# Five small moves in the hand-written order of a chunked recurrence with a maxout feed-forward: a DMA queue, a range check, a key transpose, a block of products and a weight difference

## The chip, the cores and the metric

The kernel runs on one core of one Trainium2 chip. The metric is the device time in microseconds (us) of that core. A core has five instruction streams: TensorE (PE), VectorE (DVE), ScalarE (ACT), GpSimd (POOL) and SyncE (SP). Each works through its own instructions in order. DMAs are started by instructions in such a stream; in the profile "SPq" and "ACTq" are the DMA-starting instructions of SP and ACT.

## The reference

```python
# attention: B, H, S, D = 4, 8, 768, 48
f = 1.0 / (1.0 + np.exp(-f_logit))
for t in range(S):
    state = f[:, :, t, :, None] * state + np.einsum('bhd,bhe->bhde', k[:, :, t], v[:, :, t])
    y[:, :, t] = np.einsum('bhd,bhde->bhe', q[:, :, t], state)
x = y.transpose(0, 2, 1, 3).reshape(B * S, H * D)          # 3072 x 384
# feed-forward: w1, w2, w3 are 384 x 768, w_out is 768 x 384
h = np.maximum(np.maximum(x @ w1, x @ w2), x @ w3)
out = h @ w_out
```

All inputs arrive as given by the host; the four weights come in double precision and are rounded on the chip.

## The kernel before

**Units and groups.** The recurrence is cut into 24 units of 64 time steps by two batches (128 rows of x each), numbered 0 to 23. Four units make a group of 512 rows, and the feed-forward runs group by group, six in all, one group behind the recurrence. The main loop (L1071) takes one unit u per turn, from 4 to 23. Between the steps of a turn, `fill` (L967) draws pieces of the pending feed-forward from a generator until a budget of TensorE time is used up. So one written-out order interleaves two jobs on every engine, and no scheduler changes it.

**One turn of the loop.** For unit u the turn holds: `keys(u)` (L362, four TensorE transposes of the scaled keys and a ScalarE copy, for units below 6 only) or `keys_by_blocks` (L372, 16 VectorE transposes, for the later units); `values(u-1)` (L403) and `sums(u-1)` (L424) on TensorE; `pairs(u)` (L389: 16 products on TensorE, L396, which read the scaled keys kh and queries qh of u, then a masked copy on VectorE, L399); `finish(u-1)` (L496: 16 products at L504, then three ScalarE copies at L511 into the feed-forward's input xT); the loads of later units; then the scans of unit u+1 on VectorE (L329, L347) with GpSimd's products L340 (kh) and L351 (qh).

**Loads.** From unit 6 on, f, k and q of two units are loaded together, 8 DMAs each (`load`, L183), and v of one unit by two DMAs of 96 KB (`load_v`, L164). All go through SP. In the turn of unit u, `load_v(u + 2)` follows `finish(u-1)`.

**The first group.** `ffn_first` (L797) also rounds the weights, turns the first weight, multiplies it with w_out (`linear`, L783), and before and after that moves rows of the weights between partitions: `place` (L454) starts ten DMAs for each of two `placed` tiles (L458, L465: placed<-w_in) and ten more for a third (w_in<-w_in), all on SP. GpSimd then forms sums of the placed weights, `mix_in` (L844, L850), and four differences of w_out, `mix` (L588, L592), of which `mix(1)` writes over a corner of w_out that the first group's output products (L568) still read.

**The later groups.** `inputs_by_pairs` (L869) works by a scheme with seven products instead of eight per pair of blocks. For each of three parts n it has `start`, `plain`, `sixth`, `fifth`, `seventh`, `third` and `fourth`; each adds products (L881) to one of two accumulators, A[n] in a bank of `ps_f` (p in the profile), B[n] in a bank of `ps_tr` (tr). After some of them ScalarE copies the accumulator out: L895 after start, L889 after plain, L909 after sixth, L904 after fifth. The accumulator can't be added to again before its copy is done. `sixth(0)` needs t2 and `fifth(0)` t1, which GpSimd makes in `sums_of_x` (L856, L865) from xT, once two small DMAs (`pack`, L519, L524: xT<-xT) have put the last rows of the group in place.

**Range check.** `check_range` (L273) looks, in three ScalarE steps a turn, whether the weights lie in a range: step 0 takes absolute values (L278), steps 1 and 2 are at L280. It runs from unit 10 on.

**How DMAs wait.** In the build every DMA counts up one of eight semaphores (DMAHW0 to DMAHW7) when it has landed, and a DMA instruction first waits until the DMA before it on its semaphore, in the order of the build, has landed. SP's and ACT's DMAs share the eight. A wait holds the stream it stands in.

Of the kernel before, what the change touches and what calls it, by code (L numbers as in the profile page):

```python
# [55 lines left out]
def kernel(  # L56
# [21 lines left out]
    GRP = 4  # L78
# [11 lines left out]
    def fast():  # L90
        ctx = ExitStack()
        with ctx:
# [64 lines left out]
            one = (nc.sync, nc.sync)  # L157
            both = (nc.sync, nc.scalar)
            act = (nc.scalar, nc.scalar)
# [28 lines left out]
            def load_v(u, queues=one):  # L188
                load_tokens(v_tiles[u % NLD], v, u, queues)
# [558 lines left out]
            def store_late():  # L748
                while late:
                    store(*late.pop(0))  # L750
# [46 lines left out]
            def ffn_first(xT):  # L797
                hm = new_hm()
                steps = [(j, slice(n * HALF, (n + 1) * HALF)) for n in range(2) for j in range(J_HALF)]
                steps += [(j, slice(0, TOK)) for j in range(J_HALF, NJ)]  # L800
                n_step = 0
                for j, t in steps:
                    w = t.stop - t.start
                    for i in (1, 2):
                        p = yield from product(xT, j, i, t)
                        if i == 1:
                            nc.scalar.copy(hm[:, j, t], p)
                        else:
                            nc.vector.scalar_tensor_tensor(hm[:, j, t], hm[:, j, t], 0.0, p, op0=ALU.max, op1=ALU.max)
                        round_to(ROUNDED[n_step])  # L810
                        load_weights(2, rounded[0] - 1)
                        yield (1 if w == TOK else NK) * w * COLUMN
                        n_step += 1
                        if n_step in TURNED:
                            yield from turn(TURNED[n_step])
                for a in range(NK):
                    if a < 2:
                        for n in range(2 * NK + 2):
                            place(placed[a].bitcast(FP32), w_in[a + 1], n)
                    for cost in linear(a):  # L820
                        round_to(rounded[0] + 1)
                        yield cost
                for n in range(2 * NK + 2):
                    place(w_lin, w_nat, n)
                made = iter([lambda n=n: mix_in(n) for n in range(4)] + [lambda: mix(0)])
                for i in range(GRP):
                    for n, cost in enumerate(outputs(hm, xT, i)):
                        if i or n:
                            next(made, lambda: None)()
                        if i == GRP - 1 and n == 1 and 1 in packed:  # L830
                            sums_of_x(1)
                        if i == GRP - 1 and n == 2:
                            for k in range(1, 4):
                                mix(k)
                        yield cost

# [15 lines left out]
            packed, summed = {}, {}  # L852
# [16 lines left out]
            def inputs_by_pairs(g, hm, xT):  # L869
                X = lambda k, h: halves(xT, k, h)  # L870
                t1, t2, t3, t4, t5 = sums_of_x(g)
                s1, s2, s4 = w_sum
                s3 = w_two[1][:, 0]
                COST = 2 * HALF * COLUMN
                out = lambda n, h: hm[:, 2 * n:2 * n + 2, h * HALF:(h + 1) * HALF]
                first, u3 = rests[:, 0:2, 0:HALF], tops[:, 2:4, 0:HALF]
                A, B, U5 = {}, {}, {}

                def into(b, n, w, x, begin=False):
                    for j in range(2):  # L880
                        nc.tensor.matmul(b[:, j * HALF:(j + 1) * HALF], lhsT=w[:, (2 * n + j) * 128:(2 * n + j + 1) * 128],  # L881
                                         rhs=x, start=begin and j == 0, stop=True, skip_group_check=True)

                def plain(n):
                    B[n] = bank(True)
                    into(B[n], n, w_two[0][:, 1], X(1, 0), True)
                    yield COST
                    into(B[n], n, w_two[0][:, 2], X(2, 0))
                    nc.scalar.copy(out(n, 0), two(B[n]))  # L889
                    yield COST  # L890

                def start(n):
                    A[n] = bank()
                    into(A[n], n, w_two[0][:, 0], X(0, 0), True)
                    nc.scalar.copy(first, two(A[n]))  # L895
                    yield COST

                def join(n):
                    nc.gpsimd.tensor_tensor(out(n, 0), out(n, 0), first, op=ALU.add)

                def fifth(n):
                    into(B[n], n, s1, t1, True)
                    U5[n] = two(new_top(TOK))
                    nc.scalar.copy(U5[n], two(B[n]))  # L904
                    yield COST

                def sixth(n):
                    into(A[n], n, s2, t2)
                    nc.scalar.copy(out(n, 1), two(A[n]))  # L909
                    yield COST  # L910

                def seventh(n):
                    into(A[n], n, s3, t3)
                    yield COST
                    into(A[n], n, w_two[1][:, 2], X(2, 1))
                    nc.scalar.copy(u3, two(A[n]))
                    nc.gpsimd.tensor_tensor(u3, u3, U5[n], op=ALU.add)
                    yield COST

                def third(n):  # L920
                    into(B[n], n, s4, X(1, 1))
                    yield COST
                    into(B[n], n, w_two[0][:, 2], X(2, 1))
                    nc.vector.tensor_tensor(out(n, 1), two(B[n]), out(n, 1), op=ALU.add)  # L924
                    yield COST

                def fourth(n):
                    into(A[n], n, w_two[1][:, 1], t4)
                    yield COST
                    into(A[n], n, w_two[1][:, 2], t5)  # L930
                    nc.vector.scalar_tensor_tensor(out(n, 0), out(n, 0), 0.0, two(A[n]), op0=ALU.max, op1=ALU.max)
                    nc.vector.scalar_tensor_tensor(out(n, 1), out(n, 1), 0.0, u3, op0=ALU.max, op1=ALU.max)  # L932
                    sums_of_hm(hm, n)
                    if g == 1:
                        for i in ((0, 1), (2, 3, 4), ())[n]:
                            mix_x(i)
                    yield COST

                yield from start(0)
                yield from plain(0)  # L940
                join(0)
                store_late()
                yield from sixth(0)
                yield from fifth(0)
                for n in range(1, NJ // 2):
                    yield from plain(n)
                    yield from seventh(n - 1)
                    yield from start(n)
                    join(n)
                    yield from third(n - 1)  # L950
                    yield from fifth(n)
                    yield from sixth(n)
                    yield from fourth(n - 1)
                yield from seventh(NJ // 2 - 1)
                yield from third(NJ // 2 - 1)
                yield from fourth(NJ // 2 - 1)
# [10 lines left out]
            def fill(ns):  # L967
                budget[0] += ns
                while budget[0] > 0 and pending:
                    try:  # L970
                        budget[0] -= next(pending[0])
                    except StopIteration:
                        pending.pop(0)
# [10 lines left out]
            CHECKS = 2 * GRP + 2  # L984
# [7 lines left out]
            with tc.manual_schedule():  # L992
# [78 lines left out]
                for u in range(GRP, NU):  # L1071
# [2 lines left out]
                    if n == BY_ROWS:  # L1074
                        scan(n)
                    fill(part)
                    keys(u)
                    keys_by_blocks(u, 2)
                    room_of_unit = room_of_pairs()
                    if u > GRP:  # L1080
                        values(u - 1)
                        sums(u - 1, room_of_unit)
                    pairs(u, room_of_unit)
                    if u > GRP:
                        finish(u - 1, xT)
# [12 lines left out]
                    if BY_ROWS <= u + 3 < NU and u % 2:  # L1098
                        load(u + 3, one, "fkq" if u % GRP == 1 else "f")
                    if u + 2 < NU:  # L1100
                        load_v(u + 2)
                    keys_by_blocks(u, 3)
                    if n < NU:
                        if n < BY_ROWS:
                            sigmoids(n)
                        if n != BY_ROWS:
                            scan(n)
                    check_range(u - CHECKS, 0)
                    fill(part)
                    if n < NU:  # L1110
                        after(n)
                        before(n)
                    fill(part)
                    if BY_ROWS < u + 2 < NU and u % GRP == 0:
                        load(u + 2, one, "k")
# [289 lines left out]
```

## Time and profile before

| What | Value |
|---|---|
| Time, median of 3 runs | 415.52 us (415.32 to 416.43) |
| The profiled execution's own time | 416.13 us |
| Its span in the trace | 414.4 us, TensorE clock 0.999 |
| PE busy | 393.5 us (95%) |
| DVE, POOL, ACT busy | 295.1, 246.0, 180.4 us |
| PE in 180 to 240 us | 59.62 of 60.00 us busy |
| PE in 110 to 170 us | 10.00, 9.18, 9.40, 10.00, 8.47, 9.30 of each 10.00 us |
| PE in 360 to 414 us | 49.40 of 54.00 us busy |

The span is what the trace covers; 1.7 us of the profiled execution's own time lie outside it. From about 180 us to 360 us TensorE hardly ever stands still, so a change there must shorten TensorE's own waits of some tenths. The waits of a microsecond and more lie in the first 40 us, in 120 to 165 us, where the first group of the feed-forward goes over to the second, and at the end.

In the timelines a line gives the start and the time taken in us, the engine, the source line, what is written and read, the number of instructions merged into it (a float32 product counts as two), and in brackets how long the engine stood idle before it and whom it waited for.

### The profile page before, as it was taken

The page shows a single profiled execution, that of the slowest core. Times are in us where ns is not written, and L with a number is a line of the kernel's source. Part 1 is how long each engine was busy: PE and PEld are TensorE (multiplying, and loading weights), DVE is VectorE, ACT ScalarE, POOL GpSimd, SP SyncE. Part 2 cuts the span into 40 slices and gives each one's busy share as a digit, 9 for nine tenths or more (in the row PEclk, how much of TensorE's full clock was granted, in tenths as well). Part 3 has the DMA queues.
Part 4 walks back from the last instruction along what each step waited for, and adds up shares of the span by engine and source line. Part 5 has one row for each costly group of instructions (what it writes and reads, how often), then busy time and mean ns, then how long its engine had stood idle before and what let it go on. Part 6 is the DMA issues. An engine that isn't in the chain of part 4 may idle for free.

```text
span 414.4 us, 11516 instructions
## 1 busy us (share of the span) xinstructions
PE 393.5 (95%) x4598; PEld 331.8 (80%) x4598; DVE 295.1 (71%) x569; ACT 180.4 (44%) x430; POOL 246.0 (59%) x270
## 2 busy tenths in 40 slices
PE   5988999999999989999999999999999999999995
PEld 4766765556667878998889988899988889988994
DVE  6997896997785899898899997998995550002600
ACT  2488786421223522335532345532445424586110
POOL 2189694830969777567495296577377860435700
PEclk9999999999999999999999999999999999999999
DMA  8999886676356766277645276735374003542002
GB/s 168 238 271 272 246 228 90 85 139 161 84 103 99 122 108 124 57 96 114 114 123 109 43 112 85 148 87 89 60 144 110 2 17 88 133 133 72 0 21 62
DMA packets 181562, 47.21 MB, mean 114 GB/s; under 512 B 160448, under 2 KB 179200, under 8 KB 181504
## 3 DMA queue, kind: packets, MB, share of 16 engines
q1 hardware_dynamic: 178032, 45.62, 54.1%
q10 hardware_dynamic: 3472, 0.81, 0.9%
q8 instruction: 37, 0.61, 0.6%
q14 instruction: 21, 0.17, 0.1%
HBM read 37.75 MB, written 4.72 MB: 102 GB/s over the span
## 4 chain that ended last, share of the span: by engine, by line
PE 74%; SPq 6%; POOL 5%; DVE 5%; ACT 4%; issue 2%; DMA 2%; POOLq 0%
PE p L881 15%; PE p L636 14%; PE tr L881 12%; PE tr L636 10%; PE p L542 7%; PE p L568 3%; PE p L787 3%; PE y L415 2%; SPq L164 2%; SPq L174 2%; DVE ks L382 2%; PE y L504 2%; PE a L396 2%; PE a L433 2%; POOL w_in L258 1%
## 5 line engine op out<-in xcount | busy, mean ns | idle before, releaser
L382 DVE STREAM_TRANSPOSE ks<-kh 32x128 f32<-32x128 f32 x256 | 77.4, 302 | 13.4 <-POOL kh L340 9.4
L881 PE MATMUL tr<-xT,placed 128*128 128x256 f32 x300 | 71.5, 383 | 1.1 <-ACT hm L889 1.1
L881 PEld LDWEIGHTS tr<-xT,placed 128*128 128x128 f32 x300 | 56.0, 190 | 10.4 <-ACT hm L889 2.6
L881 PE MATMUL p<-xT,placed 128*128 128x256 f32 x180 | 44.8, 380 | 1.1 <-POOL xT L865 0.8
L339 POOL COPY ends<-r 128x8 f32<-128x8 f32 x24 | 8.8, 366 | 51.1 <-DVE r L329 51.1
L881 PEld LDWEIGHTS p<-xT,placed 128*128 128x128 f32 x180 | 33.9, 190 | 6.4 <-POOL xT L865 1.2
L542 PE MATMUL p<-xT,w_in 128*128 128x256 f32 (+1 forms) x108 | 34.0, 459 | 3.4 <-POOL w_in L756 1.9
L329 DVE TENSOR_TENSOR_SCAN r<-gate,from_one 128x520 f32<-128x520 f32 x24 | 32.5, 1354 | 6.1 <-ACT gate L308 2.8
L340 POOL TENSOR_TENSOR kh<-kt,r 128x512 f32<-128x512 f32 x18 | 30.9, 1715 | 7.6 <-DVE kt L296 7.6
L511 ACT COPY xT<-y 64x256 f32<-64x256 f32 (+1 forms) x60 | 22.1, 368 | 23.2 <-PE y L504 22.5
L347 DVE TENSOR_TENSOR_SCAN prod<-gate,from_inv 128x520 f32<-128x520 f32 x24 | 31.5, 1312 | 0.0
L608 POOL TENSOR_TENSOR w_in<-hm 128x256 f32<-128x256 f32 x15 | 11.1, 739 | 32.2 <-DVE hm L932 29.4
L644 DVE TENSOR_TENSOR o<-tr,w_in 128x384 f32<-128x384 f32 (+1 forms) x11 | 5.7, 521 | 34.3 <-PE tr L636 29.8
L881 PE MATMUL p<-w_in,placed 128*128 128x256 f32 x120 | 30.0, 379 | 0.0
L542 PEld LDWEIGHTS p<-xT,w_in 128*128 128x128 f32 x108 | 19.5, 190 | 12.6 <-issue 6.0
L924 DVE TENSOR_TENSOR hm<-tr,hm 128x512 f32<-128x512 f32 x15 | 10.3, 684 | 23.1 <-ACT raw L280 17.2
L258 POOL TENSOR_TENSOR w_in<-top_bits,rest_bits 128x384 uint32<-128x384 uint32 x18 | 21.9, 1223 | 7.2 <-DVE top_bits L252 3.8
L636 PE MATMUL p<-w_in,hm 128*128 128x192 f32 x120 | 25.3, 334 | 0.6 <-ACT w_in L641 0.6
L641 ACT COPY w_in<-p 128x384 f32<-128x384 f32 x15 | 7.2, 478 | 42.1 <-PE p L636 42.1
L280 ACT ACTIVATE raw<-top_bits 128x384 f32<-128x384 f32 x48 | 25.2, 526 | 0.4
L881 PEld LDWEIGHTS p<-w_in,placed 128*128 128x128 f32 x120 | 22.8, 190 | 3.1
L636 PE MATMUL tr<-w_out,w_in 128*128 128x192 f32 x120 | 24.4, 326 | 0.0
(156 smaller groups left out, 913.7 us busy)
## 6 DMA issues: line engine op xcount, KB each, us to landing
raw<-in_moe_w_dram SPq DMA_DIRECT2D x24, 384.0 KB, 4.3
v_ld<-in_v_dram SPq DMA_DIRECT2D x48, 96.0 KB, 3.3
placed<-in_moe_w_dram SPq DMA_DIRECT2D x12, 384.0 KB, 5.7
out_dram<-o SPq DMA_DIRECT2D x46, 96.0 KB, 2.2
placed<-in_moe_w_out_dram SPq DMA_DIRECT2D x6, 384.0 KB, 5.4
f_ld<-in_f_logit_dram SPq DMA_DIRECT2D x36, 64.0 KB, 2.6
k_ld<-in_k_dram SPq DMA_DIRECT2D x36, 64.0 KB, 2.5
q_ld<-in_q_dram SPq DMA_DIRECT2D x36, 64.0 KB, 2.5
```

The lines of the kernel that those rows point to most:

```text
L258: nc.gpsimd.tensor_tensor(dst, by(top), by(rest), op=ALU.add)
L280: nc.scalar.activation(over, size, AF.Relu, scale=(-1 / HI_MIN, 1.0)[step - 1], bias=(1.0, -HI_END * (1 - 2.0 ** -24))[step - 1], accum_ou ...
L329: nc.vector.tensor_tensor_scan(r[:, 0:LEN][:, ::-1], flat(gate)[:, ::-1], flat(from_one)[:, ::-1], 1.0, op0=ALU.mult, op1=ALU.max)
L340: (nc.vector if u < BY_ROWS else nc.gpsimd).tensor_tensor(kh.rearrange("p h a t -> p a h t"), kt, by_batch(r[:, 1:LEN + 1].rearrange("p (x ...
L347: nc.vector.tensor_tensor_scan(flat(prod), flat(gate_tiles[u % 2]), flat(from_inv[u % 2]), 1.0, op0=ALU.mult, op1=ALU.max)
L382: nc.vector.transpose(ks[n * 32:(n + 1) * 32, :, par, e0:e0 + 32], kh[p0:p0 + 32, :, a, t0:t0 + 32])
L511: nc.scalar.copy(xT[o, :, t0 + a * C:t0 + (a + 1) * C], y[i, a, 0:HP * C].rearrange("p (h t) -> p h t", h=HP))
L542: nc.tensor.matmul(p if w < TOK else p.rearrange("p (two t) -> p two t", two=2), lhsT=w_in[i][:, kt, j * 128:(j + 1) * 128], rhs=x[:, t.st ...
L568: nc.tensor.matmul(p[:, 0:DM], lhsT=lhsT, rhs=rhs, start=(n == 0), stop=(n == NJ + NK - 1))
L636: nc.tensor.matmul(b[:, p * HD:(p + 1) * HD], lhsT=x, rhs=w, start=id(b) not in begun, stop=True, skip_group_check=True)
L787: nc.tensor.matmul(p[:, 0:DM], lhsT=w_in[0][:, a, j * 128:(j + 1) * 128], rhs=w_out[:, j, :], start=(j == 0), stop=(j == NJ - 1))
L881: nc.tensor.matmul(b[:, j * HALF:(j + 1) * HALF], lhsT=w[:, (2 * n + j) * 128:(2 * n + j + 1) * 128], rhs=x, start=begin and j == 0, stop= ...
```

## The change

There are five edits, all in the written order.

1. `plain(1)` is put ahead of `sixth(0)` and `fifth(0)` in each of the five later groups.
2. `check_range(u - CHECKS, 0)` is put behind the next piece of feed-forward.
3. `keys(u)` comes after `values(u-1)` and `sums(u-1)`; only unit 5 has both, so only its four transposes and the copy move.
4. `mix(1)` is put ahead of `sums_of_x(1)` on GpSimd; `mix(2)` and `mix(3)` stay behind it.
5. In the turns of units 5 to 8, `load_v` of units 7 to 10 starts its two DMAs from ScalarE's stream (`act`), right behind the three copies of `finish(u-1)`, and no longer from SP's.

```diff
--- before.py
+++ after.py
@@ -827,10 +827,12 @@
                     for n, cost in enumerate(outputs(hm, xT, i)):
                         if i or n:
                             next(made, lambda: None)()
-                        if i == GRP - 1 and n == 1 and 1 in packed:
-                            sums_of_x(1)
+                        if i == GRP - 1 and n == 1:
+                            mix(1)
+                            if 1 in packed:
+                                sums_of_x(1)
                         if i == GRP - 1 and n == 2:
-                            for k in range(1, 4):
+                            for k in range(2, 4):
                                 mix(k)
                         yield cost
 
@@ -940,10 +942,12 @@
                 yield from plain(0)
                 join(0)
                 store_late()
+                yield from plain(1)
                 yield from sixth(0)
                 yield from fifth(0)
                 for n in range(1, NJ // 2):
-                    yield from plain(n)
+                    if n > 1:
+                        yield from plain(n)
                     yield from seventh(n - 1)
                     yield from start(n)
                     join(n)
@@ -1074,12 +1078,12 @@
                     if n == BY_ROWS:
                         scan(n)
                     fill(part)
-                    keys(u)
                     keys_by_blocks(u, 2)
                     room_of_unit = room_of_pairs()
                     if u > GRP:
                         values(u - 1)
                         sums(u - 1, room_of_unit)
+                    keys(u)
                     pairs(u, room_of_unit)
                     if u > GRP:
                         finish(u - 1, xT)
@@ -1098,18 +1102,18 @@
                     if BY_ROWS <= u + 3 < NU and u % 2:
                         load(u + 3, one, "fkq" if u % GRP == 1 else "f")
                     if u + 2 < NU:
-                        load_v(u + 2)
+                        load_v(u + 2, act if GRP < u <= 2 * GRP else one)
                     keys_by_blocks(u, 3)
                     if n < NU:
                         if n < BY_ROWS:
                             sigmoids(n)
                         if n != BY_ROWS:
                             scan(n)
-                    check_range(u - CHECKS, 0)
                     fill(part)
                     if n < NU:
                         after(n)
                         before(n)
+                    check_range(u - CHECKS, 0)
                     fill(part)
                     if BY_ROWS < u + 2 < NU and u % GRP == 0:
                         load(u + 2, one, "k")
```

## The prediction

> **What bounds the kernel now.** I read the page's chain first (two of its lines), then TensorE's waits.
>
> ```profile
> span 414.4 us, 11516 instructions
> ...
> PE 74%; SPq 6%; POOL 5%; DVE 5%; ACT 4%; issue 2%; DMA 2%; POOLq 0%
> ```
>
> TensorE carries three quarters of the chain that ended last; SP's queue comes next. The waits of TensorE from 90 us on:
>
> ```profile
> PE y L504 <- ACT seen L422: 1.5, 1, 1.5
> PE tr L881 <- ACT hm L889: 1.1, 3, 0.4
> PE p L881 <- POOL xT L865: 0.8, 1, 0.8
> ```
>
> With smaller ones (0.7 on L931, 0.3 on qh, 0.3 on L895) the change-over of the first group, 120 to 165 us, holds 0.8 + 0.3 + 0.3 + 1.5 + 0.7 = 3.6 us of waits, the later groups the 1.1 us on L889. What feeds that change-over is SP's queue. Its timeline:
>
> ```profile
> 85.76 1.28 SPq L164 DMA_DIRECT2D v_ld<-in_v_dram  x2
> 87.21 1.32 SPq L458 DMA_DIRECT2D placed<-w_in  x2
> 88.58 5.06 SPq L465 DMA_DIRECT2D placed<-w_in  x8
> 93.74 1.40 SPq L164 DMA_DIRECT2D v_ld<-in_v_dram  x2
> 95.24 1.84 SPq L458 DMA_DIRECT2D placed<-w_in  x2
> 97.13 5.11 SPq L465 DMA_DIRECT2D placed<-w_in  x8
> ```
>
> One DMA starts as the last is issued, every 0.64 us: SP is limited by issuing from about 52 to 135 us. The reader is to see which DMA follows which. Then the engines that depend on it, ACT, POOL and PE, one view each:
>
> ```profile
> 95.54 1.14 ACT L511 COPY xT<-y 128x256 f32<-128x256 f32 x3 [1.23 <-PE y L504]
> ```
> ```profile
> 102.67 1.80 POOL L850 TENSOR_TENSOR placed<-placed 128x768 f32<-128x768 f32 x1 [10.86 <-DMA placed<-w_in]
> 104.41 0.19 POOL L339 COPY ends<-r 128x8 f32<-128x8 f32 x1
> 104.57 1.18 POOL L340 TENSOR_TENSOR kh<-kt,r 128x512 f32<-128x512 f32 x1
> 105.70 1.18 POOL L351 TENSOR_TENSOR qh<-qt,prod 128x512 f32<-128x512 f32 x1
> ```
> ```profile
> 108.18 0.66 PE L396 MATMUL a<-qh,kh 48*64 48x64 f32 x32
> ```
>
> POOL stands 10.86 us until the second ten placed copies are in, and kh and qh of unit 8 stand behind that sum. They end at 106.88, and TensorE uses them at 108.18: 1.30 us of slack.
>
> **What the Trainium skill says.** "DMA: Bandwidth & Descriptors", section "Issuing engines are not separate DMA queues": starting DMAs from several engines saves only the time in which a sequencer starts them. The trace has that price: 0.60 to 0.65 us for each v DMA on SP, 1.45, 1.50 and 1.43 us from the start of v of units 7, 8 and 9 to what follows. "Perfetto Trace Analysis", section "DMA Instruction — HWDGE (DVE, Sync)": the sequencer waits for semaphores before it generates descriptors, and the profiled window begins after that wait. So a DMA held by a semaphore holds everything behind it. The trace agrees: its waits list 25.7 us of SP's L269 on ACT's L280.
>
> **The change part by part.**
>
> *Plain(1) ahead of sixth(0), and the range check later.* TensorE's work is the same. Both take work from between a plain product and its use: ACT does L278 (0.56 us) ahead of L889, and TensorE waits 0.38 us for L889, three times. With two products (1.73 us) between, this goes: -1.1 us. A new tight spot: seventh(0) now has one product (0.86 us) between it and sixth(0), whose copy L909 takes 0.58 and some 0.1 us for two hand-overs: 0.18 us to spare, cost 0; 0.5 us for each of five groups if ACT is late, my upper end.
>
> *Keys of unit 5.* The four transposes stay on TensorE (0.53 us). ACT's L369 (0.47 us of ACT's order) leaves the place ahead of L422, for which L504 waited 0.71 us at 68.19: -0.46 us. The copy is used only a turn later.
>
> *Mix(1).* GpSimd is idle 3.74 us ahead of 123.18, waiting for the pack DMAs, and mix(1) takes 1.40 us. The products that read w_out end at 117.2. So it fits there, and the sums, mixes and the add L899 after it come 1.4 us earlier. This is worth something only if that pack stays where it is.
>
> *v on ACT's queue.* On ACT it costs two issues (0.70 us for the one DMA ACT issues late in the kernel), 1.3 us in each of four turns. Behind them stand L240 at 70, L791 at 83.8, L572 at 99.6 and 113.4: ACT idles 0.3 to 2.9 us there and L791's bank is wanted only at 87.7. Cost on TensorE: 0. For SP, 4.4 us of issuing leave ahead of the last pack. But the built order with its semaphores puts ACT's DMAs between SP's. Four SP instructions now wait for v DMAs to land: the 6th q copy of unit 6's load (for v of 7), the 6th k copy of unit 8's (for v of 8), the 4th placed copy of the first ten (for v of 9), the first pack of three units (for v of 10). ACT issues each only behind its L511, a point that TensorE sets. I follow the third, which decides.
>
> 1. The second wait, v of 7: issued about 69.6, landed 2.9 us later (v took 2.5 to 3.3 to land as a rule), so SP passes its 6th q copy at 72.5 and not at 66.97. The last q lands at 76.1 and not before 75.05. VectorE, busy without gap, ends the last rounding about 1.0 us later; GpSimd's L258 at 81.31 moves to about 82.4 and ends 83.4, where TensorE wanted w_out at 82.9: with keys of unit 5 counted in, +0.5 us at this point.
> 2. v of 9: L511 of that turn ends at 96.68 + 0.5 = 97.2; landed at 100.1. The 4th placed copy was issued at 89.22 (87.21 and three issues); now at 100.1.
> 3. From there to the 7th copy of the second ten are 13 issues: 13 x 0.635 = 8.3 us, so 108.4 (before: 99.67, with v of 8 and one slow issue between). That copy landed 2.97 us after its issue: 111.4. POOL's L850 starts at 111.4 and not at 102.67: +8.7.
> 4. qh of unit 8 is ready at 106.88 + 8.7 = 115.6. TensorE stands there from 108.7 and goes on at 115.65: **+7.5 us** against before.
> 5. v of 10 is issued behind the next L511, at 110.49 + 7.5 = 118.0, and lands at 120.9. SP's first pack goes then and not at 108.74. From it to the k loads of units 10 and 11 SP took 124.60 - 108.74 = 15.9 us; without v of 9 and 10 (2.9) that is 12.9 us, and 11.1 if two slow issues (1.64 and 1.35 us where 0.6 is usual) vanish. k starts between 132.0 and 133.8: +7.4 to +9.2, middle +8.3. VectorE waited 4.43 us for exactly these loads and was the chain from there to 163 us, so TensorE's shift becomes +8.3. The last pack lands at 132.0 to 133.8; the 1.4 us of mix(1) only pay back its extra lateness, and the waits of the change-over stay.
>
> Sum on the profiled execution: 416.1 + 8.3 - 1.1 = 423.3. The median of the runs shown lies 0.6 us below that execution: 415.5 + 8.3 - 1.1 = **422.7 us**.
>
> Bounds: landing of a v DMA 2.5 to 3.3 us (-0.4, +0.4), step 1 between -0.46 and +1.5 us instead of +0.5, slow issues -0.9 to +0.9, L889 and L909 -0 to +2.5. Together 420.3 to 425.3.
>
> **The rivals.**
>
> *SP is not held, and the 4.4 us count* (other side). If v of 9 had landed when SP reaches the 4th placed copy (87.8 us without v of 7), packs and loads come 4.4 us earlier, mix(1) counts, and the 3.6 us of the change-over, the 1.1 and the 0.46 go: 415.5 - 5.2 = 410.3. For it: SP is the second share of the chain. Against it: ACT can't issue v of 9 before 96. It decides from the moment at which v lands before SP's turn, which needs 12 us of shift. Chance 0.10.
>
> *Held, but taken up.* The first stall stands and part of it is made up in the change-over, because VectorE then has less pending and SP's loads run ahead: up to 3.6 us of waits vanish, 422.7 - 4.4 = 418.3 with the slow issues gone too. Against it: step 5, SP is held a second time. Chance 0.08.
>
> *ACT is held too.* v of 10 waits on ACT for the second ten placed copies to land. By step 3 these have landed by 114.5 and v of 10 comes at 118. If the copies slip further, L572 and TensorE's bank stand behind it: some 4 us, 427. Chance 0.06.
>
> **How the numbers follow.** Forecast 0.76, the rivals 0.10, 0.08 and 0.06. The range takes in the second rival and most of the forecast's upper end: 418.0 to 426.0. A measurement here can tell about 0.3% (1.2 us) from no change. Faster by more: the first rival, 0.10. Slower by more: 0.88, the rest. Within: 0.02, for a gain and a stall that meet.
>
> **What would show it.** In the changed profile SP should show gaps ahead of the 4th placed copy, which starts near 100, and ahead of the first pack, near 121. POOL's first L850 should start near 111, with a longer idle time than 10.86 us. TensorE should wait some 7 us at L396 for qh L351 near 108 to 116, and the three waits on L889 should be gone. GpSimd should run mix(1) ahead of the sums. I am wrong if SP's placed copies start before 88, or if L396 of unit 8 doesn't wait.

## The result, and the profile after

The changed kernel takes 421.62 us in the median (420.68 to 426.94, 5 runs) against 415.52 us (415.17 to 416.43, 5 runs): ratio 1.0168 with an interval of 1.0139 to 1.0198, so 6.1 us slower. The profiled execution is the one of 426.94 us; before 60 us its weights landed late (TensorE waits 2.9 us there for a copy, L780, which the profile before does not have), and it runs 4.7 us late from 57 us on, ahead of everything that was changed. I take these 4.7 us off where I compare times with before. Lines behind 833 have moved, those named here by two (L850 is now L852, L865 is L867, L881 is L883).

The page's span and its chain:

```profile
span 425.2 us, 11507 instructions
...
PE 75%; SPq 9%; DMA 5%; DVE 3%; issue 2%; POOL 2%; ACT 2%; ACTq 0%; DVEq 0%; POOLq 0%
```

SP's queue has gone from 6% to 9% of the chain. (The 5% of DMA are mostly the late weights.) TensorE's waits from 90 us on, in us: total, times, longest:

```profile
PE a L396 <- POOL qh L351: 6.8, 2, 6.3
PE y L504 <- ACT seen L422: 1.5, 1, 1.5
PE p L636 <- ACT w_in L641: 0.6, 1, 0.6
```

The three waits on L889 (1.1 us) are gone, so are those for GpSimd's sums (0.8) and on L931 (0.7); one wait of 6.3 us for qh is new. Its source is SP's timeline (start, us taken, number of DMAs):

```profile
67.13 10.06 SPq L183 DMA_DIRECT2D q_ld<-in_q_dram  x8
77.29 1.31 SPq L164 DMA_DIRECT2D v_ld<-in_v_dram  x2
78.69 4.29 SPq L183 DMA_DIRECT2D f_ld<-in_f_logit_dram  x8
83.03 8.35 SPq L183 DMA_DIRECT2D k_ld<-in_k_dram  x8
91.42 4.20 SPq L183 DMA_DIRECT2D q_ld<-in_q_dram  x8
95.80 1.33 SPq L458 DMA_DIRECT2D placed<-w_in  x2
97.18 9.83 SPq L465 DMA_DIRECT2D placed<-w_in  x8
107.12 1.22 SPq L458 DMA_DIRECT2D placed<-w_in  x2
108.38 5.05 SPq L465 DMA_DIRECT2D placed<-w_in  x8
...
123.58 1.26 SPq L524 DMA_DIRECT2D xT<-xT  x2
```

Eight DMAs take 10.06, 8.35 and 9.83 us where eight others take 4.2 to 5.1: SP stands in the middle of these three groups, and once more ahead of the pack at 123.58. No wait of TensorE names SP, but the list of what SP itself waits for does (total, times, longest):

```profile
SPq L183 <- DMA v_ld<-in_v_dram: 9.7, 2, 6.1
SPq L465 <- DMA v_ld<-in_v_dram: 5.0, 2, 4.5
SPq L524 <- DMA v_ld<-in_v_dram: 2.6, 1, 2.6
```

In the profile before SP never waits for v. The held DMAs are the ones that the prediction had named from the build's order: a q copy and a k copy (L183), a placed copy (L465) and the first pack (L524). In a narrower window the third group comes apart; its second DMA, the fourth placed copy, starts only at 102.32:

```profile
102.32 4.69 SPq L465 DMA_DIRECT2D placed<-w_in  x7
```

What SP waits for is started by ACT:

```profile
99.74 0.37 ACT L511 COPY xT<-y 128x256 f32<-128x256 f32 x1 [1.23 <-PE y L504]
99.75 0.60 ACTq L164 DMA_DIRECT2D v_ld<-in_v_dram  x1
100.13 0.37 ACT L511 COPY xT<-y 64x256 f32<-64x256 f32 x1
100.40 0.91 ACTq L164 DMA_DIRECT2D v_ld<-in_v_dram  x1
```

v of unit 9 starts at 99.75, the fourth placed copy 2.57 us later. GpSimd and TensorE follow, one view each:

```profile
114.63 1.80 POOL L852 TENSOR_TENSOR placed<-placed 128x768 f32<-128x768 f32 x1 [18.60 <-DMA placed<-w_in]
```
```profile
118.88 1.13 PE L396 MATMUL a<-qh,kh 48*64 48x64 f32 x32 [6.32 <-POOL qh L351]
119.79 1.08 PE L504 MATMUL y<-qh,state 48*48 48x64 f32 x32
120.80 3.61 PE L568 MATMUL p<-w_out,hm 128*128 128x384 f32 x6
124.24 2.10 PE L568 MATMUL p<-w_in,xT 128*128 128x384 f32 x6
```

GpSimd stands 18.60 us and not 10.86; TensorE stands 6.32 us where it had 1.30 us of slack. The first products after the stall are slow as well: L568 takes 3.61 us for six, the next six 2.10. The clock column (the fourth number) of the stretches shows it:

```profile
110.00:120.00 10.00, 3.68 (x109) 0.84 0.65 128
120.00:130.00 10.00, 10.00 (x59) 0.82 0.50 86
130.00:140.00 10.00, 10.00 (x162) 1.00 0.48 91
```

TensorE's shift against before, read from starts of the same products and less the 4.7 us:

| Place | Shift, us | Step |
|---|---|---|
| L504 in the turn of unit 5 (72.39, before 68.19) | -0.49 | -0.49, the keys |
| L396 of unit 8 (118.88, before 108.18) | +6.00 | +6.49, the stall |
| L415 of unit 8 (133.80, before 120.81) | +8.29 | +2.29, slow products |
| L415 of unit 9 (148.19, before 136.72) | +6.77 | -1.52, waits of the change-over gone |
| L415 of unit 11 (182.46, before 170.38) | +7.38 | +0.61, mostly products slow again near 167 us (+1.5), less the wait on L931 and the slow start after it (-1.1) |
| the end | +6.1 | -1.3, the waits on L889 |

They add up to 6.1 us, the difference of the medians.

### The profile page after: what moved, and what is told of

The parts are those of the page before. It is cut to its first block, busy times and chain, and to the rows that moved or that the text cites. A ratio compares the mean times of both kernels' runs of the same rounds, so it can differ in the third digit from the quotient of the medians.

```text
span 425.2 us, 11507 instructions
## 1 busy us (share of the span) xinstructions
PE 398.1 (94%) x4598; PEld 336.0 (79%) x4598; DVE 292.7 (69%) x569; ACT 180.4 (42%) x430; POOL 245.5 (58%) x270
## 4 chain that ended last, share of the span: by engine, by line
PE 75%; SPq 9%; DMA 5%; DVE 3%; issue 2%; POOL 2%; ACT 2%; ACTq 0%; DVEq 0%; POOLq 0%
PE p L883 16%; PE p L636 14%; PE tr L883 13%; PE tr L636 11%; PE p L542 6%; PE p L568 3%; DMA placed<-in_moe_w_dram 3%; PE p L787 3%; PE y L415 3%; SPq L164 2%; PE a L396 2%; PE y L504 2%; SPq L183 2%; SPq L174 2%; PE a L433 1%
## 5 line engine op out<-in xcount | busy, mean ns | idle before, releaser
L883 PE MATMUL tr<-xT,placed 128*128 128x256 f32 x300 | 71.1, 382 | 0.0
L883 PEld LDWEIGHTS tr<-xT,placed 128*128 128x128 f32 x300 | 56.3, 190 | 8.0
L883 PE MATMUL p<-xT,placed 128*128 128x256 f32 x180 | 44.6, 379 | 0.0
L883 PEld LDWEIGHTS p<-xT,placed 128*128 128x128 f32 x180 | 34.1, 190 | 4.7
L329 DVE TENSOR_TENSOR_SCAN r<-gate,from_one 128x520 f32<-128x520 f32 x24 | 31.6, 1317 | 7.8 <-ACT gate L308 4.3
L511 ACT COPY xT<-y 64x256 f32<-64x256 f32 (+1 forms) x60 | 22.1, 369 | 30.3 <-PE y L504 29.5
L883 PE MATMUL p<-w_in,placed 128*128 128x256 f32 x120 | 31.2, 391 | 0.0
L608 POOL TENSOR_TENSOR w_in<-hm 128x256 f32<-128x256 f32 x15 | 11.1, 739 | 32.3 <-DVE hm L934 32.3
L883 PEld LDWEIGHTS p<-w_in,placed 128*128 128x128 f32 x120 | 23.0, 195 | 4.7 <-issue 1.6
L258 POOL TENSOR_TENSOR w_in<-top_bits,rest_bits 128x384 uint32<-128x384 uint32 x18 | 21.4, 1199 | 9.0 <-DVE top_bits L252 4.8
L636 PE MATMUL p<-w_in,hm 128*128 128x192 f32 x120 | 25.3, 334 | 0.6 <-ACT w_in L641 0.6
L636 PE MATMUL tr<-w_out,w_in 128*128 128x192 f32 x120 | 24.4, 326 | 0.0
```

The costliest lines, as they stand in the source:

```text
L258: nc.gpsimd.tensor_tensor(dst, by(top), by(rest), op=ALU.add)
L329: nc.vector.tensor_tensor_scan(r[:, 0:LEN][:, ::-1], flat(gate)[:, ::-1], flat(from_one)[:, ::-1], 1.0, op0=ALU.mult, op1=ALU.max)
L511: nc.scalar.copy(xT[o, :, t0 + a * C:t0 + (a + 1) * C], y[i, a, 0:HP * C].rearrange("p (h t) -> p h t", h=HP))
L636: nc.tensor.matmul(b[:, p * HD:(p + 1) * HD], lhsT=x, rhs=w, start=id(b) not in begun, stop=True, skip_group_check=True)
```

## The experiments

They ran in three sets; the kernel before, run beside each, took 414.99, 414.96 and 416.32 us in the median. Ratios are to the kernel before on the same chip, and kernels of different sets are compared by them.

### The v loads alone, and everything but them

The kernel before with edit 5 alone (its difference from the changed kernel is edits 1 to 4), and the changed kernel with

```diff
-                        load_v(u + 2, act if GRP < u <= 2 * GRP else one)
+                        load_v(u + 2)
```

> The kernel before with the fifth edit alone (v of units 7 to 10 from ScalarE's stream). Theory A, SP is held by the semaphores it shares with ScalarE's DMAs: the whole stall stays and the small gains of the other edits are missing, so 422 to 424 us (ratio about 1.018), with the 4th placed copy issued only after v of 9 has landed and some 6 to 7 us of waiting at L396. Theory B, the loss comes from the reordered products and the weight difference: 415.5 us or below.

Measured 423.40 us, ratio 1.0192 (1.0178 to 1.0207).

> Edits 1 to 4 without the fifth. Theory A: no stall at L396, no wait on L889, keys of unit 5 and mix(1) count: 415.5 - 1.1 - 0.5 - 0 to 0.8 = 413.1 to 413.9 us. Theory B: slower than before, about 421 us.

Measured 414.39 us, ratio 0.9985 (0.9969 to 1.0000).

The whole loss is in edit 5. With it alone GpSimd's L850 waits 18.69 us, TensorE 6.4 us at L396, as in the changed kernel. Edits 1 to 4 bring less than expected when they stand alone: 0.6 us, which the interval hardly tells from nothing. Their waits are gone, but TensorE's waits from 90 us on begin with a new one:

```profile
PE a L396 <- POOL qh L351: 1.7, 1, 1.7
PE y L504 <- ACT seen L422: 1.5, 1, 1.5
PE p L636 <- DVE hm L933: 0.7, 1, 0.7
```

This qh is that of unit 10. SP starts its k loads at 124.72 us (before: 124.60), VectorE stands 4.20 us for them, and TensorE, which is 1.9 us earlier than before at 136 us, now waits for what comes of them and is 0.45 us earlier at 138. SP's loads took back most of what the four edits had given up to there. The later groups give 1.3 us more, so this trace ends 1.7 us before that of the kernel before; the medians differ by 0.6 us only.

### The same v loads from GpSimd's stream

```diff
-                        load_v(u + 2, act if GRP < u <= 2 * GRP else one)
+                        load_v(u + 2, (nc.gpsimd, nc.gpsimd) if GRP < u <= 2 * GRP else one)
```

In the build, GpSimd's DMAs count on semaphores of their own.

> The changed kernel with v of units 7 to 10 started from GpSimd's stream at the same places; GpSimd's DMAs count up semaphores of their own, so SP waits for none of them. Theory A: SP runs on, 4.4 us ahead at the last pack, and the kernel comes to 410 to 413 us[...]. Theory C, the loss comes from v transfers that run at another time and collide with the others on the same DMA engines: as slow as the changed kernel, about 421 us.

Measured 409.56 us, ratio 0.9863 (0.9848 to 0.9878): 1.4% faster than before, the best of all and a little below the range of theory A. SP isn't held, and everything behind is early:

```profile
87.65 5.03 SPq L465 DMA_DIRECT2D placed<-w_in  x8
...
106.66 1.26 SPq L524 DMA_DIRECT2D xT<-xT  x2
...
116.02 1.31 SPq L524 DMA_DIRECT2D xT<-xT  x2
...
119.53 5.23 SPq L183 DMA_DIRECT2D k_ld<-in_k_dram  x8
```

The last pack comes at 116.02 (before 120.33), the k loads at 119.53 (124.60). From 90 us on TensorE waits 0.8 us in all. SP's list of waits has none for v. Yet v of unit 9 starts from GpSimd only at 91.19 us and takes 4.2 us to land, when SP has already started all of its first ten placed copies (the last before 92.68). So it isn't an earlier v that frees SP: SP no longer waits for it. Nor is the loss a collision of transfers: in the changed kernel v of unit 9 landed faster (2.57 us), and yet that kernel is the slow one. Taking v off SP is worth what the first rival said, once nothing holds SP.

The kernel before with this one line and without edits 1 to 4:

> The kernel before with one thing changed: v of units 7 to 10 comes from GpSimd's queue; the other four edits are left out. With them the same move gave 409.56 us, and the four edits alone 414.39 against 414.99, 0.6 us. Theory S (the four edits save 1.6 us of waits on TensorE, but only where SP's loads are not what is waited for next): without them this kernel is 1.6 us slower than 409.56, 411.2 us (410.6 to 411.8), with the three waits on L889 (1.1 us) and the one on L422 ahead of L504 at 68 us back in the trace. Theory N (they are worth 0.6 us or less wherever they stand): 409.6 to 410.2.

Measured 411.91 us, ratio 0.9926 (0.9910 to 0.9941), just above the range of theory S. The three waits on L889 (1.1 us) and the one ahead of L504 (0.7) are back. So the four edits are worth 0.6% (0.9926 against 0.9863), some 2.6 us, where SP's loads are early, and 0.6 us where they are not. I had expected 1.6, and the traces of these two kernels differ by just that (410.1 and 408.5 us); where the rest of the 2.6 comes from is not shown.

### One load at a time

v of unit 9 back on SP:

```diff
-                        load_v(u + 2, act if GRP < u <= 2 * GRP else one)
+                        load_v(u + 2, act if GRP < u <= 2 * GRP and u != 7 else one)
```

> The changed kernel with v of unit 9 back on SP; v of 7, 8 and 10 stay on ScalarE. Theory A: the 4th placed copy is no longer held, only the 6th q and 6th k copies are, so GpSimd's first L850 sum comes about 3 us later than before instead of 8 to 9, and TensorE waits about 2 us at L396: 415.5 + 2 - 1.5 = 415 to 418 us. Theory D, the cost is ScalarE's own time for issuing: three quarters of the loss stays, about 420 us.

Measured 418.39 us, ratio 1.0075 (1.0060 to 1.0091), above the range of theory A; half of the loss is left, less than theory D had. The eight placed copies are down to 5.95 us (from 9.83) and the stall at L396 to 2.4, as expected; but a wait of 2.7 us for GpSimd's sums is new:

```profile
PE p L883 <- POOL xT L867: 2.7, 1, 2.7
PE a L396 <- POOL qh L351: 2.4, 1, 2.4
```

The sums wait for the last pack, which SP starts at 125.35: it still stands ahead of the first pack, for v of unit 10.

v of units 7 and 8 alone on ACT (`u in (5, 6)`):

> The changed kernel, with only v of units 7 and 8 left on ScalarE's queue, v of 9 and 10 back on SP's. SP's q copies of unit 6 and its k copies of unit 8 are still held (10 us in place of 5 for eight). Theory A (a hold costs only where something on TensorE's path waits for what is behind it; these two have slack) expects the time of the four edits without any v moved, 414.4 us (413.8 to 415.2). The rival, that each hold costs about what the two others do (some 3 us each: 6.1 us for all), expects 417 to 420.

Measured 417.79 us, ratio 1.0063 (1.0048 to 1.0078). Here my theory's expectation failed, and the time lies in the range of its rival. TensorE stands 2.6 us at L396 for qh of unit 8. SP's copies show why:

```profile
64.31 8.27 SPq L183 DMA_DIRECT2D q_ld<-in_q_dram  x8
72.68 1.31 SPq L164 DMA_DIRECT2D v_ld<-in_v_dram  x2
74.09 5.46 SPq L183 DMA_DIRECT2D f_ld<-in_f_logit_dram  x8
79.59 6.91 SPq L183 DMA_DIRECT2D k_ld<-in_k_dram  x8
```

Without v on ACT these groups take 5.17, 4.29 and 5.11 us. The two holds delay no load that is wanted soon, but all that SP has queued behind them: the first L852 starts at 106.42 and not at 102.31. I had asked who needs the held copies, not who needs what is queued dozens of DMAs later.

v of unit 9 alone on ACT (`u == 7`):

> The changed kernel with only v of unit 9 left on ScalarE's queue; v of 7, 8 and 10 on SP's. In the built order SP's second placed copy of the first ten waits for v of 9. Theory A (the stall is set by the moment at which v of 9 lands, whatever SP did before): ScalarE can issue v of 9 at 95.5 us, landed by 98.5; from SP's second placed copy to the seventh of the second ten are 15 issues, 15 x 0.635 = 9.5 us, landed 3 us later, 111.0; qh 4.1 us later, 115.1, TensorE stands 6.5 us: 420.5 to 422.5 us. Additive theory (each hold costs its own share; that of v of 9 is what the changed kernel took over the kernel with v of 9 back, 3.2 us): 414.4 + 3.2 = 417.6 us.

Measured 422.69 us, ratio 1.0167 (1.0138 to 1.0195), just above the range of theory A: the whole loss from one load, so the costs of the holds don't add up as the rival had it. SP comes to its second placed copy early and stands there, 10.6 us for v by its list of waits:

```profile
86.34 11.90 SPq L458 DMA_DIRECT2D placed<-w_in  x2
98.65 5.01 SPq L465 DMA_DIRECT2D placed<-w_in  x8
103.75 1.40 SPq L164 DMA_DIRECT2D v_ld<-in_v_dram  x2
```

TensorE's stall is 9.3 us and not the 6.5 that I expected: I left out the v load of unit 8 that stands between the two tens of placed copies here (1.51 us with its gap), one issue in the second ten was 1.0 us slow, and TensorE came to the stall 0.7 us sooner. Units 7 and 8 cost 0.8% over the kernel without moved v (1.0063 against 0.9985), unit 9 1.8%, all four 1.8% (1.5% in a second run of the changed kernel, on the chip of this one, ratio 1.0136). What counts is when the last held DMA ahead of the placed copies goes, whatever SP did before.

Much is made up again. At L415 of unit 8 (120.81 us before) TensorE is 12.6 us further behind than ahead of the stall, at L415 of unit 11 (170.38 us before) 7.9 us: every wait of the change-over is gone. The second rival's mechanism is real, though not strong enough.

v of units 11 to 14 on ACT, those of 7 to 10 on SP (`8 < u <= 12`):

> The changed kernel with v of units 11 to 14 on ScalarE's queue, those of 7 to 10 back on SP's: as many DMAs moved, later. ScalarE's work is the same kind as in the changed kernel. Held in SP's order are only late k copies of units whose loads are early; the placed copies and the packs of the change-over are not. Theory A expects 414.4 us (413.5 to 415.5), the time of the four edits alone. If the cost lay in ScalarE issuing DMAs between its copies, it would be near 420.

Measured 414.50 us, ratio 0.9997 (0.9978 to 1.0016), not told apart from the kernel with no v moved. As many DMAs in ScalarE's stream cost nothing here. SP was held all the same: its list has 8.5 us for v ahead of a load of the range check (L269, which I had not named) and 2.0 us at L183. So neither issuing from ScalarE nor a hold of SP costs anything in itself; it depends on what stands behind the held DMA. In the turns of units 5 to 8 ScalarE's own time isn't the cause either: two DMAs, v of unit 9, make the whole loss, and from 90 us on TensorE waits for ScalarE in the changed kernel only where it did before (L504, L636).

### The slow products after the stall

```diff
+                    if u == 8:
+                        busy(14)
                     pairs(u, room_of_unit)
```

`busy` issues products that nothing reads.

> The changed kernel with 14 products of 128x256 that nothing reads put ahead of the pairs of unit 8, to keep TensorE occupied in the stall of 6.3 us there (14 x 0.43 = 6.0 us). If the slower granted clock after that stall (0.82 to 0.84 for about 15 us, and again near 165 us) comes of standing idle, the stall stays as long as it was and the products after it run at their usual times (L568 2.1 us and not 3.6): 418.5 to 420 us. If the lower clock has another cause, 421 to 422; if the 14 products only delay what could have run, over 422.

> The changed kernel once more, on the same chip and beside the products in its stall, to size what TensorE's slower clock after the stall costs: 421.6 us (420.7 to 422.5), with a stall of 6.3 us at L396 for qh of unit 8. If its first profiled execution, longer by 5 us from before 60 us, was typical, 425.

> The 14 products in the stall once more, on the same chip as the changed kernel. If the slower clock after the stall costs the 2 us that the one profile suggests: 2 us below the changed kernel. If only what the medians gave: 0.7 us below it.

Measured: with the products 420.90 us, ratio 1.0133 (1.0113 to 1.0152), between the two ranges of the expectation; on another chip 420.57 us, ratio 1.0107 (1.0087 to 1.0127), where the changed kernel took 421.79 us (421.72 to 422.23), ratio 1.0136 (1.0117 to 1.0156). The trace of this second execution of the changed kernel, with no late weights, has the same stall and the same slow products:

```profile
114.05 1.13 PE L396 MATMUL a<-qh,kh 48*64 48x64 f32 x32 [6.46 <-POOL qh L351]
115.96 3.36 PE L568 MATMUL p<-w_out,hm 128*128 128x384 f32 x6
119.16 2.10 PE L568 MATMUL p<-w_in,xT 128*128 128x384 f32 x6
```

With the products in the stall, on that chip:

```profile
108.14 6.31 PE L983 MATMUL p<-from_one,ident 128*128 128x256 f32 x28
114.75 0.69 PE L396 MATMUL a<-qh,kh 48*64 48x64 f32 x32 [0.30 <-POOL qh L351]
115.83 2.20 PE L568 MATMUL p<-w_out,hm 128*128 128x384 f32 x6
117.86 2.10 PE L568 MATMUL p<-w_in,xT 128*128 128x384 f32 x6
```

L396 doesn't start earlier in its turn, since qh is as late as before, but L568 takes 2.20 us, in both traces with the products. From L415 of unit 7, ahead of the stall, to L415 of unit 8 the changed kernel takes 22.39 and 22.28 us in its two traces, with the products 20.38 and 20.36. So TensorE's idle time in this stall brings the slow products, 2 us. The time of the kernel gains less: by the ratios 0.35% and 0.29%, some 1.4 and 1.2 us, with intervals that overlap those of the changed kernel. In the last trace TensorE then waits 2.3 us at L883 for GpSimd's sums, and part of the 2 us goes there: one DMA of the packs landed 3.6 us after its issue, where the other trace with the products, which has no such wait, shows 2.6 us at most. Where the rest goes is not shown.

Slow products don't follow every short stall: the 2.6 us with v of units 7 and 8 on ACT were followed by a L568 of 3.72 us, the 2.4 us with v of 9 back on SP by one of 2.20. The slow products near 167 us come behind a wait of 1.55 us at L504, and the kernel before has the same wait (1.53 us) with products at their usual time behind it. What decides this stays open.

## Why the prediction was right, and where not

The forecast was 422.7 us, with one mechanism: DMAs on ACT's stream hold SP through shared semaphores, and the placed copies, GpSimd's sum, qh and TensorE follow. That is what the trace shows, and the experiments bear it out: edit 5 alone makes the loss, v of unit 9 alone makes it, and the same loads on other semaphores make a gain. By its steps:

- **Edits 1 and 2, -1.1 us.** Right: the waits on L889 are gone, the later groups give 1.3 us. The feared wait of `seventh` on ScalarE's copy didn't come.
- **Edit 3, -0.46 us.** Measured -0.49.
- **Edit 4, nothing.** Right for the changed kernel: mix(1) runs in GpSimd's idle time ahead of the sums, which wait 2.94 us more for the late pack all the same.
- **Step 1, +0.5 us by the late q load. Wrong.** Nothing followed from it: GpSimd's last L258 starts at 85.53 us, which is 80.83 less the 4.7 (before 81.31), 0.48 us early like TensorE. The late q load wasn't what the rounding waited for.
- **Step 2, v of 9 issued at 97.2, fourth placed copy at 100.1.** The copy went at 97.6, 2.5 us sooner. Of these, 0.99 are step 1; 1.1 come of the place of the issue, since I had put it behind the three copies L511, and it runs beside the first of them (99.75 beside 99.74); the rest is the landing, 2.57 us and not 2.9.
- **Step 3, 8.3 us of issues and a landing.** 8.61 us (102.32 to 110.93, with a second stop of 0.4 us for the other half of v), and the landing took 3.70 us to L852, not 2.97. L852 at 109.9, said 111.4.
- **Step 4, TensorE +7.5 us at L396.** +6.0. Of the 1.5 us that are missing, 0.99 are step 1; the earlier issue and landing of step 2 (1.4 us) are mostly taken up by the slower issues and the longer landing of step 3 (1.0 us).
- **Step 5, the first pack at 120.9, k loads +8.3 us, and the waits of the change-over stay. Wrong in size and in what follows.** The pack went at 118.9 and the k loads at 130.8, +6.2 us, below the range of +7.4 to +9.2: the time between them was as forecast (11.95 us, said 11.1 to 12.9), but the pack was 2 us earlier than I had it. Meanwhile TensorE had become 8.3 us late by its slow products. So the loads, less late than TensorE, no longer set its shift; 1.5 us of the change-over's waits went, where I had 0.8 us more.
- **Not in the prediction:** TensorE's slow products after the stall, +2.3 us, and again 1.5 us near 167 us.
- **The bounds.** The parts that are listed add up to 427.5 us at the upper end (422.7 + 0.4 + 1.0 + 0.9 + 2.5), not to 425.3. The upper end of the range, 426.0, was thus lower than these parts allow; what was measured lies well below it.

By terms: 7.5 + 0.8 - 1.1 was forecast, 6.0 + 2.3 - 1.5 + 0.6 - 1.3 came. That the total is near (7.2 and 6.1 us) is in part luck: an unforeseen loss stands in the place of one that I made too large.

Of the rivals, the first had the right size for a kernel in which SP isn't held (410.3 said, 409.56 with GpSimd). The second came in part, 1.5 us of it. The third didn't come: ACT is not held, its v of unit 10 starts as soon as its L511 does. What the Trainium skill states in "Perfetto Trace Analysis", section "DMA Instruction — HWDGE (DVE, Sync)", that the sequencer itself waits for semaphores, ahead of the window that the profile shows, agrees with SP's timeline here: at 97.8 us SP stands for 4.5 us, and it starts nothing that is behind the waiting DMA.

## What to carry to other kernels

When a DMA goes to another engine's stream, look at which semaphores it shares in the build and which DMA of the old stream comes next on them: that DMA waits until the moved one has landed, and everything queued behind it waits too. Ask who needs the DMAs queued behind the held one, not only who needs the held one. Against the same kernel with all v on SP (ratio 0.9985), the eight DMAs cost 1.8% from ScalarE and gave 1.2% from GpSimd, so here the stream was to be chosen by its semaphores and by when it can issue, not by which engine has the most idle time: GpSimd was busier than ScalarE (246.0 and 180.4 us before). Whether ScalarE would do as well with an earlier issue, or with semaphores of its own, was not run. Look first at what the queue that starts DMAs waits for itself: its own list named the held DMAs and the cause.

## What was not expected of the hardware

- A DMA that stands behind copies in ScalarE's order starts beside the first of them (99.75 us beside a copy of 0.37 us at 99.74), not behind its end.
- After an idle time of 6.3 to 6.5 us TensorE's granted clock was lower (0.84 and 0.82 in two stretches of 10 us in one execution of the changed kernel, 0.66 in one in the other), and six products took 3.36 to 3.61 us instead of 2.10; after the 9.3 us with v of unit 9 alone on ACT they took 4.21. With products in the idle time they took 2.20.
- A stop of SP in its queue isn't listed as a wait on the engines that suffer from it: L396 names qh and L852 names the placed DMA. The 9.83 us for eight DMAs show the stop, and only SP's own waits (L465, 4.5 us) say that it is for v.
